# A transformer block on one core: the front rewritten as a list of 140 steps, with several query projections open at once

## The chip, the core and the metric

The kernel runs on one core of one Trainium2 chip. The metric is the device time of one execution in microseconds (us), the median of several runs. One profiled execution gives the trace; its engines are called PE (the matrix engine), PEld (its weight loads), DVE (vector), ACT (scalar), POOL (GpSimd) and SP (which issues most DMAs).

## The reference

One pre-norm block on x of 2048 rows and 448 columns: attention with 16 query heads of 28 columns that share one key and one value head, then a gated FFN of 1792 columns.

```python
x = A_x
h = x + _A_ref(_layernorm(x), wq, wk, wv, wo)
# q = x@wq (16 heads), k = x@wk, v = x@wv, p = softmax(q k / sqrt(28)), (p v) @ wo
h2 = h + _B_ref(_layernorm(h), w1, w3, w2)
# (silu(x@w1) * (x@w3)) @ w2
```

## The kernel before, in words

Everything is computed in a split form: a value is a high part (fp32r) and a low part (the rest), and a product is three matmuls, high by high, low by high, high by low. For 448 rows of contraction that makes 11 matmuls of 512 columns a projection (`mm_D`): three high by high, three low by high, three high by low, and two for the last 64 rows.

x is cut into four quarters t of 512 rows, each of four blocks n of 128 rows. The **front**, of which this case is, does for each quarter: statistics on DVE (`stats`), the power -0.5 on POOL (`ln_rstd`), the scaling (`ln_norm`, on DVE or, with a bias that POOL prepares, on ACT), a small copy on POOL, 16 transposes on PE (`ln_tr`, four chunks c, one PSUM bank each; ACT copies the high part out, DVE subtracts for the low part), one joint projection for key and value (`kv`), and four query projections g (`q(t, g)`), one for four heads. ACT copies a finished projection to SBUF (tile QR); `q(0, 0)` goes straight to the tile QS with a DVE subtraction. `va` transposes the values back; `k_low` makes the keys' low part; `k_diff` on POOL subtracts the keys of neighbouring quarters (tile kd). The query weight is split in four chunks: its high part on ACT, its low part on POOL (`split_wq`, `low_wq`).

Between the projections stand 20 **quads**: the row maxima of the scores for the first steps of the attention. A quad is four matmuls of 32 rows side by side into four banks. A quad "D" multiplies with kd, and ACT writes its relu to SBUF; the quad "U" after it multiplies with the keys KH, and DVE adds the relu and takes the maximum (`both`, line 281). So a pair D, U covers two quarters of the keys for four heads.

There are eight PSUM banks, given out first freed, first taken (`bank`, `done`). ACT, DVE and POOL run what stands in the program in its order, so the order in which the code is written is the order on each of them, and PE waits wherever its next bank, weight or moving operand is not there. In the kernel before, the order is written as calls: `kv` and `q` run their 11 matmuls in one go, with at most one quad after the sixth (`between`).

After the front comes the **main loop** (attention, 256 steps), and then the FFN. `load_wo` clears a tile and loads the output weight; `split_wo` splits it in steps 1, 3, 5 and 7 of the main loop.

Of the kernel before, what the change touches and what calls it, by code (L numbers as in the profile page):

```python
# [38 lines left out]

@with_exitstack  # L40
def block_kernel(
# [98 lines left out]

    def mm_D(ps, lhs, rhs, lsl, rsl, between=None, part=False, lows_last=False):


# [4 lines left out]
        if lows_last:  # L150
            terms.insert(6, terms.pop(9))
        for k, (a, ca, b, cb) in enumerate(terms):
            pe.matmul(  # L153
                ps, lhs[b][:, cb, lsl], rhs[a][:, ca, rsl],
                start=(k == 0), stop=(k == len(terms) - 1 and not part),
            )
            if between is not None and k == 5:
                between()
# [34 lines left out]
    def ln_norm(t, n, eng=ve):  # L193
        _, mv, rs, xns, nb = LN[t]
        xn = xns[n] = ln_pool.tile([P, 512], F32, name="xn", bufs=4)
        if eng is se:
            se.activation(xn[:, :D], X[t][:, n], AF.Identity, bias=nb[:, n : n + 1], scale=rs[:, n : n + 1])
        else:
            eng.tensor_scalar(xn[:, :D], X[t][:, n], mv[:, n, 0:1], rs[:, n : n + 1],
                              op0=ALU.subtract, op1=ALU.mult)  # L200
# [4 lines left out]
    def ln_tr(t, c, ffn=False, dve=False, between=None):  # L205

        ps = bank()
        if c == 0:
            XT[t] = (xt_pool.tile([P, 4, T], F32R, name="xh"), xt_pool.tile([P, 4, T], F32R, name="xl"))
        xh, xl = XT[t]  # L210
        xns = LN[t][3]
        for n in range(NQ):
            pe.transpose(ps[:, n * P : (n + 1) * P], xns[n][:, c * P : (c + 1) * P], ident)  # L213
            if between is not None and n < NQ - 1:
                between()

        def copy(o, i):
            if dve:
                ve.tensor_copy(o, i)
            else:  # L220
                se.activation(o, i, AF.Copy)
# [8 lines left out]
        if c < 3:  # L230
            ve.tensor_tensor(xl[:, c], ps, f(xh[:, c]), op=ALU.subtract)
        else:
            ve.tensor_tensor(xh[64:128, 3], ps[64:128], f(hi[64:128, 3]), op=ALU.subtract)
# [211 lines left out]
    def low_wq(c0, c1, eng):
        for c in range(c0, c1 + 1):
            eng.tensor_tensor(WQ[1][:, c, :, :DH], wq4[:, c], f(WQ[0][:, c, :, :DH]), op=ALU.subtract)

    def split_wq(c0, c1, eng=None):
        for c in range(c0, c1 + 1):  # L450
            se.activation(WQ[0][:, c, :, :DH], wq4[:, c], AF.Copy)
            if eng:
                low_wq(c, c, eng)
# [16 lines left out]
    def norm(t, eng):  # L470
        for n in range(NQ):
            ln_norm(t, n, eng)

    def tr(t, *cs):
        for c in cs or range(4):
            ln_tr(t, c)

    def kv(t, between=None):
        cols = slice(t * T, (t + 1) * T)
        ps = bank()  # L480
        mm_D(ps[:96], WKV, XT[t], slice(0, 96), slice(0, T), between)
        se.activation(KH[0:64, cols], ps[0:64], AF.Identity, bias=kb)
        vt = VT[:, t % 2]
        se.activation(vt[64:96], ps[64:96], AF.Copy)
        sy.dma_start(f(KH[64:128, cols]), f(KH[0:64, cols]))
        return vt, ps

    def k_diff(t):
        ge.tensor_tensor(KD[:, t // 2], f(KH[:, t * T : (t + 1) * T]), f(KH[:, (t - 1) * T : t * T]),
                         op=ALU.subtract)  # L490

    def k_low(t, ps):
        cols = slice(t * T, (t + 1) * T)
        ve.scalar_tensor_tensor(KL[0:64, cols], ps[0:64], kb, f(KH[0:64, cols]), op0=ALU.add, op1=ALU.subtract)
        sy.dma_start(f(KL[64:128, cols]), f(KL[0:64, cols]))
        done(ps)

    def va(t, vt):
        ps = bank()
        for n in range(NQ):  # L500
            pe.transpose(ps[:, 32 * n : 32 * n + 32], vt[64:96, n * P : (n + 1) * P], ident[64:96, 64:96])
# [4 lines left out]
    def q(t, g, between=None):
        ps = bank()
        mm_D(ps, [w[:, :, 4 * g : 4 * g + 4].rearrange("p c h r -> p c (h r)") for w in WQ],
             XT[t], slice(0, P), slice(0, T), between, lows_last=True)
        if t == g == 0:  # L510
            build_qs(0, ps)
        else:
            se.activation(QR[t][:, g], ps, AF.Copy)
        done(ps)

    first = [(quad, i, n, 0, diff) for i, n in ((0, 0), (0, 1), (0, 2), (0, 3), (1, 0)) for diff in (True, False)]
    first += [(quad, 0, n, 1, diff) for n in range(NQ) for diff in (True, False)]
    first += [(max_done, 0), (max_out, 0)]
    first += [(quad, 1, 0, 1, diff) for diff in (True, False)]

    def quads(n=1):
        while n > 0 and first:
            fn, *args = first.pop(0)
            fn(*args)
            n -= fn is quad
# [10 lines left out]
    tr(0, 1, 2, 3)
    split_wq(0, 3)
    low_wq(0, 3, ge)
    v0, p0 = kv(0)
    stats(1)  # L540
    k_low(0, p0)
# [5 lines left out]
    stats(2)
    k_diff(1)
    k_low(1, p1)
    q(0, 2)  # L550
    norm(2, ve)
    q(0, 3)
    va(0, v0)
    va(1, v1)
    build_qs(1)
    quads()
    q(1, 0, quads)
    quads()
    tr(2)
    v2, p2 = kv(2, quads)  # L560
    stats(3, True)
    quads()
    q(1, 1, quads)
# [1 line left out]
    k_low(2, p2)
    va(2, v2)
    quads()
    q(1, 2, quads)
    quads()
    q(1, 3)  # L570
    build_qs(2)
    quads()
    tr(3)
    v3, p3 = kv(3)
    k_diff(3)
# [1 line left out]
    q(2, 0)
    k_low(3, p3)
    va(3, v3)
    q(2, 1)  # L580
    for t, g in ((2, 2), (2, 3), (3, 0), (3, 1)):
        quads()
        q(t, g, quads)
    quads()
    q(3, 2, quads)
    q(3, 3)
    quads(64)
# [227 lines left out]
```

## Time and profile before

| | |
|---|---|
| median of three runs | 1194.07 us (1192.97 to 1194.17) |
| the profiled execution's own time | 1192.15 us |
| its span in the trace | 1190.4 us |
| mean granted clock of PE | 1.00 |
| PE, first key and value projection starts | 11.40 us |
| PE, first matmul of the main loop starts | 90.06 us |

A line of the timeline has start, length, engine, source line, operation, output and inputs, and a count of equal instructions that follow one another; in brackets the idle time before it and what ended it. The lengths of matmuls are modelled and overlap, so the pace of PE is read from start to start.

### The profile page before, as it was taken

The numbers are of one execution on the slowest core, as the hardware profiler recorded it, in microseconds if no ns is written. First come the engines' busy times: TensorE is split into PE (matmuls) and PEld (weight loads), VectorE is DVE, ScalarE is ACT, GpSimd is POOL, SyncE is SP. The second block draws the span as 40 slices with busy tenths as digits, with TensorE's granted clock in tenths as the row PEclk, the third lists the DMA queues.
The fourth block names the chain that finished last, engine by engine and source line by source line (L and its number), as shares of the span: only waits on it lengthen the run. The fifth ranks groups of instructions, "written<-read, shape, count | busy, mean of one in ns | idle before, by whom it ended". The sixth has DMA issues, their size and how long they took to land. (4 is left out here: it accounts for less than half of the span.)

```text
span 1190.4 us, 24122 instructions
## 1 busy us (share of the span) xinstructions
PE 1175.1 (99%) x9594; PEld 727.5 (61%) x9594; DVE 812.0 (68%) x1482; ACT 726.3 (61%) x1381; POOL 332.5 (28%) x258
## 2 busy tenths in 40 slices
PE   9999999999999999999999999999999999999998
PEld 7564444445544445444445443688888888888886
DVE  7758999998898997899997982254444445444333
ACT  4759999997799996899996999411211111111111
POOL 4201101110101110110111032363555455445552
PEclk9999999999999999999999999999999999999999
DMA  5010101000001000010000010114000000000000
GB/s 174 12 37 2 34 2 47 11 12 2 10 13 36 11 12 2 11 46 10 4 12 10 3 46 11 40 45 117 1 32 1 1 1 31 1 1 32 1 1 32
DMA packets 32377, 26.92 MB, mean 23 GB/s; under 512 B 10824, under 2 KB 28936, under 8 KB 32264
## 3 DMA queue, kind: packets, MB, share of 16 engines
q1 hardware_dynamic: 31704, 25.32, 7.2%
q8 instruction: 75, 1.23, 0.4%
q14 instruction: 38, 0.31, 0.1%
q10 hardware_dynamic: 560, 0.06, 0.0%
HBM read 20.25 MB, written 3.80 MB: 20 GB/s over the span
## 5 line engine op out<-in xcount | busy, mean ns | idle before, releaser
L328 ACT ACTIVATE pt<-pb 128x512 f32<-128x512 f32 x1024 | 531.7, 612 | 11.3 <-PE pb L318 6.0
L273 DVE TENSOR_REDUCE mx<-pa 128x1 f32<-128x512 f32 x708 | 461.0, 684 | 52.8 <-PE pb L318 37.0
L318 PE MATMUL pb<-qs,KH 32*128 32x512 f32 x2048 | 342.9, 431 | 0.1
L267 PE MATMUL pa<-KH,qs 32*128 32x512 f32 x866 | 327.4, 487 | 0.4 <-ACT relu L277 0.4
L336 PE MATMUL po<-pt,VA 128*32 128x256 f32 (+1 forms) x2984 | 298.1, 471 | 5.7 <-ACT OT L340 5.3
L318 PE MATMUL pb<-qs,KL 32*128 32x512 f32 x1024 | 283.6, 419 | 0.0
L318 PEld LDWEIGHTS pb<-qs,KH 32*128 32x128 f32 x2048 | 174.5, 182 | 113.7 <-DVE mx L273 49.8
L153 PE MATMUL pa<-xh,w 128*128 128x512 f32 x784 | 202.1, 391 | 0.0
L707 ACT ACTIVATE rb<-pa 128x512 f32<-128x512 f32 x56 | 30.5, 596 | 251.3 <-PE pa L699 251.3
L153 PEld LDWEIGHTS pa<-xh,w 128*128 128x128 f32 x784 | 146.1, 188 | 30.3 <-issue 1.2
L267 PEld LDWEIGHTS pa<-KH,qs 32*128 32x128 f32 x866 | 142.2, 181 | 10.7 <-issue 2.4
L724 PE MATMUL pb<-w2s,hid 128*128 128x448 f32 x672 | 143.9, 370 | 0.7 <-POOL w2s L390 0.7
L318 PEld LDWEIGHTS pb<-qs,KL 32*128 32x128 f32 x1024 | 136.9, 182 | 2.5
L724 PEld LDWEIGHTS pb<-w2s,hid 128*128 128x128 f32 x672 | 123.9, 188 | 20.4 <-issue 10.1
L336 PEld LDWEIGHTS po<-pt,VA 128*32 128x32 f32 x2984 | 58.8, 108 | 122.1 <-issue 104.9
L277 ACT ACTIVATE relu<-pa 128x512 f32<-128x512 f32 x158 | 91.1, 600 | 52.7 <-PE pa L267 34.0
L281 DVE CUSTOM_DVE_ANT_0 relu<-pa,relu 128x512 f32<-128x512 f32 x158 | 105.6, 682 | 16.3 <-ACT relu L277 12.9
L382 POOL TENSOR_TENSOR w<-QR,w 128x1024 fp32r<-128x1024 f32 x32 | 84.3, 2647 | 94.4 <-PE pa L699 80.8
L716 DVE TENSOR_TENSOR hid<-rb,hid 128x512 fp32r<-128x512 f32 x56 | 72.5, 1295 | 39.2 <-ACT hid L715 39.2
L360 POOL TENSOR_TENSOR OT<-OT,rb 128x512 f32<-128x512 f32 x16 | 20.5, 1283 | 274.3 <-DMA rb<-sd 81.3
L153 PE MATMUL pa<-xl,w 128*128 128x512 f32 x336 | 94.6, 390 | 0.0
L381 DVE CAST w<-QR 128x1024 fp32r<-128x1024 f32 x32 | 22.2, 694 | 90.2 <-PE pa L153 82.0
(99 smaller groups left out, 954.9 us busy)
## 6 DMA issues: line engine op xcount, KB each, us to landing
rb<-sd SPq DMA_DIRECT2D x64, 64.0 KB
QR<-in_B_w_dram SPq DMA_DIRECT2D x16, 192.0 KB
X<-in_A_x_dram SPq DMA_DIRECT2D x3, 896.0 KB
...
qs<-ngt SPq DMA_DIRECT2D x64, 2.0 KB
sm<-OT SPq DMA_DIRECT2D x64, 2.0 KB
```

The source lines that it names most:

```text
L153: pe.matmul(ps, lhs[b][:, cb, lsl], rhs[a][:, ca, rsl], start=(k == 0), stop=(k == len(terms) - 1 and not part),)
L267: pe.matmul(self.ps, QS[i][r, 0, n * P : (n + 1) * P], ks[r], start=True, stop=True)
L273: ve.tensor_reduce(self.col(), self.ps, axis=AX.X, op=ALU.max)
L277: se.activation(r, self.ps, AF.Relu)
L281: ve.tensor_tensor_reduce(r, self.ps, r, 1.0, LOW, op0=ALU.add, op1=ALU.max, accum_out=self.col())
L318: pe.matmul(self.ps, (KH, KH, KL)[k][r, c * P : (c + 1) * P], QS[i][r, (0, 1, 0)[k]], start=(k == 0), stop=(k == 2))
L328: se.activation(pt, self.ps, AF.Exp, bias=0.0, scale=SCALE)
L336: pe.matmul(PO[i][32 * j : 32 * j + 32, q], VA[:, c], PT[i, c, j][:, q], start=(c == 0 and h0 == 0), stop=(c == NC - 1 and h1 == 2))
L382: ge.tensor_tensor(wl, W13[k], f(wh), op=ALU.subtract)
L707: se.activation(sg, ps[0], AF.Silu)
L716: ve.tensor_tensor(h[:, 1], sg, f(h[:, 0]), op=ALU.subtract)
L724: pe.matmul(Y[t][n][:, :D], hid[a][:, n * P : (n + 1) * P], w2s[:, b, :D], start=(k == 0 and m == 0), stop=(k == NF - 1 and m == 2))
```

## The change

The front after the first chunk of the first quarter's transposes is written as one list, `FRONT`, whose names call small functions: `tr.t.c` the transposes of a chunk, `wh`, `wp`, `wv` the split of the query weight (high on ACT, low on POOL, low on DVE), `ka.t` and `kb.t` the first six and the last five matmuls of a key and value projection, `qa.t.g` and `qb.t.g` the same of a query projection, `st` statistics, `na` and `nm` the scaling on ACT and on DVE, `kl`, `kd`, `va`, `qs` as before, `D` and `U` the quads, `mx` the maxima of the first four heads. A projection takes its bank at `qa` and keeps it until ACT has copied it out after `qb`. The matmuls themselves and their number are the same.

```diff
+FRONT = """
+tr.0.1 tr.0.2 tr.0.3 wh.1 wh.0 ka.0 wp.0 wh.2 wp.1 st.1.1 kb.0 wh.3 wv.3 na.1.0 na.1.1 wv.2 qa.0.0
+na.1.2 qa.0.1 na.1.3 st.2.1 qa.0.2 qb.0.0 qa.0.3 qb.0.2 qb.0.3 tr.1.0 tr.1.1 tr.1.2 tr.1.3 na.2.0
...
-    def mm_D(ps, lhs, rhs, lsl, rsl, between=None, part=False, lows_last=False):
+    def mm_D(ps, lhs, rhs, lsl, rsl, part=False, lows_last=False, half=None):
...
+            if half is None or half == (k > 5):
+                pe.matmul(
...
+    def wq_high(c):
+        se.activation(WQ[0][:, c, :, :DH], wq4[:, c], AF.Copy)
+
+    def wq_low(eng, c):
+        eng.tensor_tensor(WQ[1][:, c, :, :DH], wq4[:, c], f(WQ[0][:, c, :, :DH]), op=ALU.subtract)
...
+    def q(half, t, g):
+        if not half:
+            PP[t, g] = bank()
+        ps = PP[t, g]
         mm_D(ps, [w[:, :, 4 * g : 4 * g + 4].rearrange("p c h r -> p c (h r)") for w in WQ],
-             XT[t], slice(0, P), slice(0, T), between, lows_last=True)
...
+             XT[t], slice(0, P), slice(0, T), lows_last=True, half=half)
+        if half:
...
+            done(PP.pop((t, g)))
...
+        "tr": ln_tr, "st": stats, "nm": ln_norm, "na": lambda t, n: ln_norm(t, n, se), "np": lambda t, n: ln_norm(t, n, ge),
+        "wh": wq_high, "wp": lambda c: wq_low(ge, c), "wv": lambda c: wq_low(ve, c),
+        "ka": lambda t: kv(False, t), "kb": lambda t: kv(True, t), "kl": k_low, "kd": k_diff, "va": va,
+        "qa": lambda t, g: q(False, t, g), "qb": lambda t, g: q(True, t, g), "qs": build_qs,
...
-    norm(1, ve)
-    q(0, 0)
-    q(0, 1)
-    tr(1)
-    v1, p1 = kv(1)
...
-    norm(3, se)
...
+    for op in FRONT:
+        name, *args = op.split(".")
+        front[name](*map(int, args))
     load_wo()
...
-        at(1 + 2 * g, split_wo, g)
+        at(5 + 2 * g, split_wo, g)
```

On PE, behind the first key and value projection, stood the query projections of the first quarter one whole after the other. The rows give output bank and inputs; xh and xl are the high and low part of the transposed x, OS0 and OS1 those of the query weight, and the number behind pb tells one bank's use from another's.

```order
L153 MATMUL pb_311<-xh_208,OS0_103 128x512 x3
L153 MATMUL pb_311<-xl_209,OS0_103 128x512 x3
L153 MATMUL pb_311<-xh_208,OS0_103 128x512
L153 MATMUL pb_311<-xh_208,OS1_104 128x512 x4
L153 MATMUL pb_326<-xh_208,OS0_103 128x512 x3
L153 MATMUL pb_326<-xl_209,OS0_103 128x512 x3
L153 MATMUL pb_326<-xh_208,OS0_103 128x512
L153 MATMUL pb_326<-xh_208,OS1_104 128x512 x4
```

The same place on PE now:

```order
L164 MATMUL pb_305<-xh_208,OS0_103 128x512 x3
L164 MATMUL pb_305<-xl_209,OS0_103 128x512 x3
L164 MATMUL pb_315<-xh_208,OS0_103 128x512 x3
L164 MATMUL pb_315<-xl_209,OS0_103 128x512 x3
L164 MATMUL pb_340<-xh_208,OS0_103 128x512 x3
L164 MATMUL pb_340<-xl_209,OS0_103 128x512 x3
L164 MATMUL pb_305<-xh_208,OS0_103 128x512
L164 MATMUL pb_305<-xh_208,OS1_104 128x512 x4
L164 MATMUL pb_355<-xh_208,OS0_103 128x512 x3
L164 MATMUL pb_355<-xl_209,OS0_103 128x512 x3
L164 MATMUL pb_340<-xh_208,OS0_103 128x512
L164 MATMUL pb_340<-xh_208,OS1_104 128x512 x4
```

Three projections are begun, 18 matmuls, before the first matmul that reads the low part of the weight.

On ACT, from the first key copy (KH) to the second quarter's first high part (the second xh), stood:

```order
L482 ACTIVATE KH_93<-pb_269,small_85 64x512
L484 ACTIVATE vt_118<-pb_269 32x512
L248 ACTIVATE qs_323<-pb_311 128x512
L513 ACTIVATE QR0_96<-pb_326 128x512
L221 ACTIVATE xh_340<-pb_339 128x512
```

and stands now, with the scaling of the second quarter (xn, from X1) and one chunk of the weight (OS0):

```order
L484 ACTIVATE KH_93<-pb_263,small_85 64x512
L486 ACTIVATE vt_118<-pb_263 32x512
L455 ACTIVATE OS0_103<-OT_102 128x16x28
L206 ACTIVATE xn_298<-X1_78,rs_273 128x448
L206 ACTIVATE xn_301<-X1_78,rs_273 128x448
L206 ACTIVATE xn_312<-X1_78,rs_273 128x448
L206 ACTIVATE xn_322<-X1_78,rs_273 128x448
L257 ACTIVATE qs_352<-pb_305 128x512
L517 ACTIVATE QR0_96<-pb_340 128x512
L517 ACTIVATE QR0_96<-pb_355 128x512
L230 ACTIVATE xh_375<-pb_374 128x512
```

The four scalings stand ahead of the copies that free the banks of the projections; their bias (rs) comes from POOL. The third quarter is scaled on ACT too, between its other work, and the fourth, which was scaled on ACT, is scaled on DVE.

On PE, the last quarter's transposes (xn to pb) stood behind a U quad (KH, qs) and ahead of the key and value projection (wkvs):

```order
L267 MATMUL pa<-KH,qs 128x512 x4
L213 MATMUL pb<-ident,xn 128x128 x16
L153 MATMUL pb<-xh,wkvs 96x512 x3
L153 MATMUL pb<-xl,wkvs 96x512 x3
L153 MATMUL pb<-xh,wkvs 96x512 x5
L153 MATMUL pb<-xh,OS_103 128x512 x3
```

They stand now so, where the first wkvs projection is that of the third quarter and the second that of the fourth:

```order
L276 MATMUL pa<-KH,qs 128x512 x4
L502 MATMUL pb<-ident,vt 128x32 x4
L222 MATMUL pb<-ident,xn 128x128 x12
L164 MATMUL pb<-xh,wkvs 96x512 x3
L164 MATMUL pb<-xl,wkvs 96x512 x3
L222 MATMUL pb<-ident,xn 128x128 x4
L164 MATMUL pb<-xh,wkvs 96x512 x5
L276 MATMUL pa<-kd,qs 128x512 x4
L164 MATMUL pb<-xh,wkvs 96x512 x3
L164 MATMUL pb<-xl,wkvs 96x512 x3
L164 MATMUL pb<-xh,wkvs 96x512 x5
```

Between the last quarter's transposes and the projection that reads them now stand a projection of another quarter and a D quad.

More of the change, by code (lines that the diff above doesn't have):

```diff
@@ L37 @@
               "6a 7a 5c 4a 4b 6b 7b").split()
+FRONT = """
+tr.0.1 tr.0.2 tr.0.3 wh.1 wh.0 ka.0 wp.0 wh.2 wp.1 st.1.1 kb.0 wh.3 wv.3 na.1.0 na.1.1 wv.2 qa.0.0
+na.1.2 qa.0.1 na.1.3 st.2.1 qa.0.2 qb.0.0 qa.0.3 qb.0.2 qb.0.3 tr.1.0 tr.1.1 tr.1.2 tr.1.3 na.2.0
+qb.0.1 ka.1 na.2.1 qs.2 na.2.2 kb.1 na.2.3 qa.1.0 kl.0 st.3 qa.1.2 tr.2.0 tr.2.1 tr.2.2 tr.2.3
+qb.1.2 kd.1 nm.3.0 qb.1.0 nm.3.1 va.1 D.0.0.0 kl.1 qa.1.1 U.0.0.0 qb.1.1 nm.3.2 D.0.1.0 qa.1.3
+nm.3.3 U.0.1.0 qb.1.3 D.0.2.0 qa.2.0 U.0.2.0 qs.1 va.0 tr.3.0 tr.3.1 tr.3.2 ka.2 tr.3.3 kb.2 kl.2
+D.0.3.0 ka.3 kb.3 kl.3 kd.3 qb.2.0 U.0.3.0 qa.2.3 D.1.0.0 qb.2.3 U.1.0.0 qa.3.2 D.0.0.1 qb.3.2
+U.0.0.1 qa.3.1 D.0.1.1 qb.3.1 U.0.1.1 qa.3.3 D.0.2.1 qb.3.3 U.0.2.1 qa.2.1 D.0.3.1 qb.2.1 U.0.3.1
+mx.0 qa.3.0 va.3 D.1.0.1 qb.3.0 va.2 U.1.0.1 qa.2.2 qb.2.2
+""".split()
 @with_exitstack
@@ L152, in mm_D @@
         for k, (a, ca, b, cb) in enumerate(terms):
[L153 to L158, printed above, removed]
+            if half is None or half == (k > 5):
+                pe.matmul(
+                    ps, lhs[b][:, cb, lsl], rhs[a][:, ca, rsl],
+                    start=(k == 0), stop=(k == len(terms) - 1 and not part),
+                )
     def load_w(dst, w, eng=sy):
@@ L443, in block_kernel @@
     wq4 = wq_r.rearrange("p c (h r) -> p c h r", h=H)
[L445 to L453, printed above, removed]
+    def wq_high(c):
+        se.activation(WQ[0][:, c, :, :DH], wq4[:, c], AF.Copy)
+    def wq_low(eng, c):
+        eng.tensor_tensor(WQ[1][:, c, :, :DH], wq4[:, c], f(WQ[0][:, c, :, :DH]), op=ALU.subtract)
     def load_wo():
@@ L468, in stats, with kv @@
         ln_rstd(t, nbias=nbias)
[L470 to L486, printed above, removed]
+    PP, VV = {}, {}
+    def kv(half, t):
+        if not half:
+            PP[t] = bank()
+        ps = PP[t]
+        mm_D(ps[:96], WKV, XT[t], slice(0, 96), slice(0, T), half=half)
+        if half:
+            cols = slice(t * T, (t + 1) * T)
+            se.activation(KH[0:64, cols], ps[0:64], AF.Identity, bias=kb)
+            vt = VV[t] = VT[:, t % 2]
+            se.activation(vt[64:96], ps[64:96], AF.Copy)
+            sy.dma_start(f(KH[64:128, cols]), f(KH[0:64, cols]))
     def k_diff(t):
@@ L490, in k_diff, with k_low @@
                          op=ALU.subtract)
-    def k_low(t, ps):
-        cols = slice(t * T, (t + 1) * T)
+    def k_low(t):
+        cols, ps = slice(t * T, (t + 1) * T), PP.pop(t)
         ve.scalar_tensor_tensor(KL[0:64, cols], ps[0:64], kb, f(KH[0:64, cols]), op0=ALU.add, op1=ALU.subtract)
@@ L496, in k_low, with va @@
         done(ps)
-    def va(t, vt):
-        ps = bank()
+    def va(t):
+        ps, vt = bank(), VV.pop(t)
         for n in range(NQ):
@@ L504, in va, with maxima @@
         done(ps)
-    def q(t, g, between=None):
-        ps = bank()
+    def q(half, t, g):
+        if not half:
+            PP[t, g] = bank()
+        ps = PP[t, g]
         mm_D(ps, [w[:, :, 4 * g : 4 * g + 4].rearrange("p c h r -> p c (h r)") for w in WQ],
-             XT[t], slice(0, P), slice(0, T), between, lows_last=True)
[L510 to L525, printed above, removed]
+             XT[t], slice(0, P), slice(0, T), lows_last=True, half=half)
+        if half:
+            if t == g == 0:
+                build_qs(0, ps)
+            else:
+                se.activation(QR[t][:, g], ps, AF.Copy)
+            done(PP.pop((t, g)))
+    def maxima(i):
+        max_done(i)
+        max_out(i)
+    front = {
+        "tr": ln_tr, "st": stats, "nm": ln_norm, "na": lambda t, n: ln_norm(t, n, se), "np": lambda t, n: ln_norm(t, n, ge),
+        "wh": wq_high, "wp": lambda c: wq_low(ge, c), "wv": lambda c: wq_low(ve, c),
+        "ka": lambda t: kv(False, t), "kb": lambda t: kv(True, t), "kl": k_low, "kd": k_diff, "va": va,
+        "qa": lambda t, g: q(False, t, g), "qb": lambda t, g: q(True, t, g), "qs": build_qs,
+        "D": lambda i, n, kp: quad(i, n, kp, True), "U": lambda i, n, kp: quad(i, n, kp, False), "mx": maxima,
+    }
     for n in range(NQ):
@@ L535, in block_kernel @@
     done(warm)
[L536 to L541, printed above, removed]
-    norm(1, ve)
-    q(0, 0)
-    q(0, 1)
-    tr(1)
-    v1, p1 = kv(1)
[L547 to L563, printed above, removed]
-    norm(3, se)
[L565 to L575, printed above, removed]
-    load_wo()
[L577 to L587, printed above, removed]
+    for op in FRONT:
+        name, *args = op.split(".")
+        front[name](*map(int, args))
+    load_wo()
     free.remove(7)
```

## The prediction

> **What bounds the kernel now.** The page comes first:
>
> ```profile
> span 1190.4 us, 24122 instructions
> PE 1175.1 (99%) x9594; PEld 727.5 (61%) x9594; DVE 812.0 (68%) x1482; ACT 726.3 (61%) x1381; POOL 332.5 (28%) x258
> ```
>
> PE is the bound, but 99% overstates it, since the lengths of matmuls overlap. So I read PE's timeline of the front from start to start, first where nothing else seems to hold it up, for prices, then where it stands.
>
> ```profile
> 14.41 0.84 PE L153 MATMUL pb<-xh,OS 128*128 128x512 f32 x3
> ...
> 17.50 1.20 PE L153 MATMUL pb<-xh,OS 128*128 128x512 f32 x4 [0.60 <-POOL OS L447]
> ...
> 20.36 1.91 PE L213 MATMUL pb<-ident,xn 128*128 128x128 f32 x16
> 22.02 1.12 PE L153 MATMUL pb<-xh,wkvs 128*96 128x512 f32 x3
> ...
> 30.16 0.49 PE L501 MATMUL pb<-ident,vt 32*128 32x32 f32 x5
> ...
> 37.67 1.45 PE L153 MATMUL pb<-xh,wkvs 128*96 128x512 f32 x3 [0.65 <-ACT xh L221]
> ...
> 41.75 0.50 PE L267 MATMUL pa<-kd,qs 32*128 32x512 f32 x4
> ...
> 46.89 1.72 PE L267 MATMUL pa<-kd,qs 32*128 32x512 f32 x3 [0.28 <-DVE mx L281]
> ...
> 51.18 0.50 PE L267 MATMUL pa<-KH,qs 32*128 32x512 f32 x1 [0.37 <-ACT relu L277]
> ...
> 52.99 0.51 PE L267 MATMUL pa<-kd,qs 32*128 32x512 f32 x4
> ...
> 60.00 1.67 PE L153 MATMUL pb<-xl,wkvs 128*96 128x512 f32 x3 [0.60 <-DVE xl L231]
> ...
> 62.66 0.85 PE L153 MATMUL pb<-xh,OS 128*128 128x512 f32 x3
> ...
> 65.25 0.43 PE L501 MATMUL pb<-ident,vt 32*128 32x32 f32 x4
> 65.61 0.97 PE L153 MATMUL pb<-xh,OS 128*128 128x512 f32 x3
> ...
> 68.35 0.50 PE L267 MATMUL pa<-kd,qs 32*128 32x512 f32 x4
> ...
> 70.39 0.51 PE L267 MATMUL pa<-KH,qs 32*128 32x512 f32 x4
> ...
> 74.23 0.51 PE L267 MATMUL pa<-KH,qs 32*128 32x512 f32 x4
> ...
> 90.06 0.49 PE L267 MATMUL pa<-KH,qs 32*128 32x512 f32 x1
> ```
>
> Prices: the 11 matmuls of a projection take 65.25 - 62.66 = 2.59 us, 0.235 each; 16 transposes 22.02 - 20.36 = 1.66; a value transpose (`va`) 65.61 - 65.25 = 0.36. From 70.39 to 74.23 stand 11 matmuls and two quads, so a quad costs (3.84 - 2.59) / 2 = 0.625.
>
> Now the stretches, time taken less work at these prices. 14.41 to 20.36, 22 matmuls: 5.95 - 5.17 = 0.78. To 30.16, 16 transposes and 33 matmuls: 9.80 - 9.42 = 0.38. To 41.75, two `va`, four quads, 22 matmuls, 16 transposes: 11.59 - 10.05 = 1.54. To 52.99, four quads, one `va`, 22 matmuls: 11.24 - 8.03 = 3.21. To 62.66, two quads, 16 transposes, 22 matmuls: 9.67 - 8.08 = 1.59. To 68.35, 22 matmuls and a `va`: 0.16. To 90.06, ten quads and 66 matmuls: -0.05. So PE stands 7.6 us in the front, nearly all before 62.66, and the last third is dense. That is all a new order of the front can win: its work stays the same.
>
> **The change part by part.** PE's work from 14.41 on: 209 matmuls x 0.235 = 49.1, 48 transposes 5.0, four `va` 1.4, 20 quads 12.5, in all 68.0. If PE never waits, the main loop starts at 14.41 + 68.0 = 82.4 instead of 90.06. I follow the new list along PE at these prices and ask at each place whether what it needs is there. The rows for the other engines:
>
> ```profile
> 21.05 2.06 ACT L221 ACTIVATE xh<-pb 128x512 fp32r<-128x512 f32 x4
> 31.28 2.05 ACT L277 ACTIVATE relu<-pa 128x512 f32<-128x512 f32 x4
> 47.93 2.72 ACT L197 ACTIVATE xn<-X,rs 128x448 f32<-128x448 f32 x4 [1.11 <-POOL rs L191]
> ```
>
> ```profile
> 12.97 4.48 POOL L447 TENSOR_TENSOR OS<-OT,OS 128x448 fp32r<-128x448 f32 x4 [2.05 <-ACT OS L451]
> 46.27 1.01 POOL L188 TENSOR_TENSOR rs<-rs,small 128x4 f32<-128x4 f32 x1 [13.23 <-DVE rs L187]
> 65.92 1.29 POOL L489 TENSOR_TENSOR kd<-KH 128x512 fp32r<-128x512 f32 x1 [7.17 <-DMA KH<-KH]
> ...
> 95.42 1.14 POOL L463 TENSOR_TENSOR WO<-OT,WO 128x448 fp32r<-128x448 f32 x1 [26.68 <-DVE WO L462]
> ```
>
> ```profile
> 13.65 0.63 DVE L182 BATCH_NORM_STATS2 st<-X 128x6 f32<-128x448 f32 x1
> ...
> 16.71 0.76 DVE L187 TENSOR_SCALAR rs<-mv 128x4 f32<-128x4 f32 x1
> ...
> 21.67 1.89 DVE L231 TENSOR_TENSOR xl<-pb,xh 128x512 fp32r<-128x512 f32 x3 [0.69 <-ACT xh L221]
> 23.59 0.69 DVE L233 TENSOR_TENSOR xh<-pb,xh 64x512 fp32r<-64x512 f32 x1
> ...
> 28.68 2.74 DVE L199 TENSOR_SCALAR xn<-X,mv,rs 128x448 f32<-128x448 f32 x4 [0.36 <-POOL rs L188]
> ...
> 74.86 0.69 DVE L281 CUSTOM_DVE_ANT_0 relu<-pa,relu 128x512 f32<-128x512 f32 x1 [1.31 <-ACT relu L277]
> ...
> 75.48 0.69 DVE L281 CUSTOM_DVE_ANT_0 relu<-pa,relu 128x512 f32<-128x512 f32 x1
> ...
> 94.95 0.39 DVE L462 CAST WO<-OT 128x448 fp32r<-128x448 f32 x1
> ```
>
> ```profile
> 63.57 0.46 SPq L485 DMA_DIRECT2D KH<-KH  x1
> ```
>
> *The weight's low part (0.78 before).* POOL made its four chunks one after the other, 1.12 us each, and PE waited. Now 18 matmuls (4.2 us) go first, to 18.6. POOL begins half a us later than its 12.97, with the second chunk that ACT makes, and its two end at about 15.7. DVE's two stand behind the statistics (13.65 to 16.71) and the small operation after them, at about 16.9. Their duration no row shows for this form; the same operation with both inputs in SBUF elsewhere:
>
> ```profile
> L716 DVE TENSOR_TENSOR hid<-rb,hid x56: 691/1242/2718, 767.8 to 1179.0; 128x512 fp32r<-128x512 f32 x56
> ```
>
> For 448 columns that is 0.60 to 2.38, by the median 1.09 us. I take the median, because POOL works beside it here as there: done at 19.1, needed at 18.6 + 3 x 0.235 = 19.3, so nothing is lost. At the upper end they are done at 21.7 and PE loses 2.4 us.
>
> The rows show DVE held up by POOL: the scalar operation at 16.71 took 0.76 us and ended with POOL's last chunk (12.97 + 4.48 = 17.45), and four scalings at 28.68 took 2.74. [...]
>
> *The scaling of the second and third quarter on ACT.* Its bias leaves POOL 47.93 - 46.27 = 1.66 us after the power starts, so ACT scales from 16.9 + 1.7 = 18.6 to 21.25 (four in 2.65). Behind it in ACT's queue wait the copies of q(0, 0), q(0, 2), q(0, 3). Who waits for those: the transposes `tr.1.3` take q(0, 0)'s bank at 24.8, which DVE releases at about 23.1, behind the third quarter's statistics (19.1 + 3.1, then two operations). And `tr.1.0` needs the scaled rows at 23.6. So 1.7 us of slack; beyond that every us of delay is one on PE. The third quarter's last scaling ends at 31.2, its transposes start at 31.8.
>
> *Second quarter's transposes (0.38 before).* The last half of a projection, 1.2 us, now lies between them and `ka.1`; ACT (four chunks in 2.06) and DVE (0.63 a chunk) are done in time.
>
> *Third quarter (1.54 and most of 3.21 before).* Here quads, transposes and statistics met: between 30.16 and 52.99 DVE had sixteen `both` (75.48 - 74.86 = 0.62 each), 3.1 us of statistics (13.65 to 16.71) and 2.6 of low parts (1.89 + 0.69) to do, and quads waited for its banks. Now the statistics of the last quarter and the third's transposes (31.8 to 33.5) come before the first quad (36.2), behind them two half projections. POOL's kd for it is ready at 34.
>
> *Fourth quarter (1.59 before).* The transposes come at 47; between them and `ka.3` at 52 lie 2.6 us of `ka.2` and `kb.2` and a quad, while DVE, busy with a U quad's four `both` (from 46.7) and a copy until 49.4, finishes the low parts at 51.4. This is tight: `ka.2` needs a bank that DVE frees at about 48.0, just when PE comes. I allow 0.5 us. The keys' copy by DMA takes 65.92 - 63.57 = 2.35 us; kd is ready near 59, the quad that needs it comes at 61.
>
> *Last third.* One projection and two quads in 3.84 us, as before: ACT needs five operations of about 0.5 and DVE 4 x 0.62 = 2.5 of that, and DVE idles 1.31 a pair. Nothing changes; the steps before it only come earlier.
>
> *The output weight's load and split* go behind the front; main-loop steps 5 to 11 instead of 1 to 7 still come before the tile is overwritten in step 16. I cost this at nothing; DVE and POOL do 4 x 0.39 and 4 x 1.14 us of it beside PE. Without that cover it would cost a PE wait of one such split, 1.1 us.
>
> Sum: 7.6 us of waits go, 0.6 come back (0.5 at the fourth quarter, 0.1 at the low parts): 7.0. Against the profiled execution's 1192.15 us that is 1185.2; the three runs' median is 1.9 above that execution, so 1194.07 - 7.0 = 1187.1. A measurement of this kernel can tell about 0.2% (2.4 us) from no change.
>
> **The rivals.** *Half of it comes back (faster still).* The tight places all miss: low parts 2.4, ACT's scaling 1, the fourth quarter's chain 1.2. Then 7.6 - 4.6 = 3.0 is won: 1191.1. For it: margins of 0.2 to 1.7 us on durations from other places. Against: the first two depend on DVE being at its slowest.
>
> *The main loop takes it back.* If its first steps wait for DVE, which does its last `both` 1.2 us closer to it (11 matmuls behind the last U quad instead of 16), a gain would end there: 1192 to 1196, taken as 1193.5. Against: DVE stood idle before its first reduction there:
>
> ```profile
> 90.59 3.84 DVE L273 TENSOR_REDUCE mx<-pa 128x1 f32<-128x512 f32 x6 [1.69 <-PE pa L267]
> ```
>
> 1.69 us covers 1.2, and nothing later hangs on a fixed time.
>
> *Slower: the quads run out of banks.* One or two projections hold a bank while each quad takes four of eight; `U.0.0.1` takes the bank that `U.1.0.0`'s last `both` frees, only 0.4 us ahead by my count. If each of 20 quads waited one `both` (0.62), 12.4 us come against the 7.6: 1194.07 + 4.8 = 1198.9. The break-even is 0.38 us a quad (7.6 / 20); slower by over 0.2% it is from 0.5 on. Against: a pair of D and U takes nine banks in turn before and after alike, and the dense stretch before shows DVE idle in each pair.
>
> **How the numbers follow.** Forecast 0.68, its own range 1185.6 to 1188.9; half back 0.18; taken back 0.09; slower 0.05. Faster by over 0.2% are the first two, 0.86; the third is within 0.2%: 0.09; slower 0.05. The range goes from 1185.0 (all 7.6 us, and 1.5 more if 209 matmuls are priced 0.007 us too high) to 1192.0, which takes in the half.
>
> **What would show it.** Right: PE's first main-loop matmul at 82.5 to 83.5 us, no bracketed wait of PE in the front over 0.5 us, the first low-part matmul about 18.6 without a wait, the last third again at 3.84 a pair, and the main loop as long as before (1190.4 - 90.06 = 1100.3). Wrong: PE waiting for DVE's OS or for ACT's xn at 19 to 25 (the first rival's terms), pairs of quads longer than 4.2 us, or a main loop longer by what the front saved.

## The result, and the profile after

| | before | after |
|---|---|---|
| median | 1193.52 us (1192.73 to 1194.17, 4 runs) | 1183.36 us (1183.27 to 1183.48, 4 runs) |
| profiled execution, own time / span | 1192.15 / 1190.4 us | 1183.29 / 1181.5 us |
| first query projection starts | 14.41 us | 14.05 us |
| main loop's first matmul | 90.06 us | 81.16 us |
| from there to the end of the span | 1100.3 us | 1100.3 us |

The ratio is 0.992, with a 95% interval from 0.9908 to 0.9931: faster, and by more than forecast (1187.1, range 1185.0 to 1192.0). By their times, two of the four executions of before in the table (1194.07 and 1194.17) are of a slower kind that the new kernel does not show and that the experiments take up. (The list has 111 names; the title's 140 is a miscount.)

The page of after, its first lines:

```profile
span 1181.5 us, 24119 instructions
PE 1169.5 (99%) x9594; PEld 726.5 (61%) x9594; DVE 809.2 (68%) x1480; ACT 729.5 (62%) x1385; POOL 330.0 (28%) x258
```

PE's timeline of after, columns as before (start, length, engine, line, operation, tiles, count):

```profile
14.05 0.85 PE L164 MATMUL pb<-xh,OS 128*128 128x512 f32 x3
...
18.14 1.98 PE L164 MATMUL pb<-xh,OS 128*128 128x512 f32 x8
...
22.90 1.91 PE L222 MATMUL pb<-ident,xn 128*128 128x128 f32 x16
24.57 1.40 PE L164 MATMUL pb<-xh,OS 128*128 128x512 f32 x5
...
45.78 1.53 PE L222 MATMUL pb<-ident,xn 128*128 128x128 f32 x12
47.14 0.95 PE L164 MATMUL pb<-xh,wkvs 128*96 128x512 f32 x3
...
50.73 0.94 PE L164 MATMUL pb<-xh,wkvs 128*96 128x512 f32 x3
...
60.45 0.50 PE L276 MATMUL pa<-kd,qs 32*128 32x512 f32 x4
...
64.27 0.50 PE L276 MATMUL pa<-kd,qs 32*128 32x512 f32 x4
...
81.16 0.50 PE L276 MATMUL pa<-KH,qs 32*128 32x512 f32 x1
```

No row between 14 and 82 us ends in a bracket, where before had five. The second of the eight matmuls at 18.14 is the first that reads the low part of the weight, and nothing holds it up. The front took 81.16 - 14.05 = 67.11 us against 75.65: PE is dense from end to end. The other engines at the places that the prediction walks through, first ACT of after:

```profile
18.61 2.72 ACT L206 ACTIVATE xn<-X,rs 128x448 f32<-128x448 f32 x4 [2.40 <-POOL rs L200]
21.35 0.60 ACT L257 ACTIVATE qs<-pb 128x512 fp32r<-128x512 f32 x1
```

DVE of after:

```profile
16.45 1.16 DVE L458 TENSOR_TENSOR OS<-OT,OS 128x448 fp32r<-128x448 f32 x2
...
48.41 1.88 DVE L240 TENSOR_TENSOR xl<-pb,xh 128x512 fp32r<-128x512 f32 x3
```

POOL of after:

```profile
16.59 1.36 POOL L197 TENSOR_TENSOR rs<-rs,small 128x4 f32<-128x4 f32 x1 [1.26 <-DVE rs L196]
...
21.59 1.04 POOL L197 TENSOR_TENSOR rs<-rs,small 128x4 f32<-128x4 f32 x1
```

DVE's two low parts end at 17.6 (forecast 19.1; PE comes to them at about 18.8); ACT's scaling starts at 18.6, as walked; the last quarter's low parts end at 50.3, ahead of the projection at 50.73.

### The profile page after: what moved, and what is told of

Read it like the earlier page. It is cut to its first block, busy times and chain, and to the rows that moved or that the text cites. A ratio compares the mean times of both kernels' runs of the same rounds, so it can differ in the third digit from the quotient of the medians.

```text
span 1181.5 us, 24119 instructions
## 1 busy us (share of the span) xinstructions
PE 1169.5 (99%) x9594; PEld 726.5 (61%) x9594; DVE 809.2 (68%) x1480; ACT 729.5 (62%) x1385; POOL 330.0 (28%) x258
```

## The experiments

Theory W (waits) is the prediction's: the gain is what PE stood in the front, each stand can be given back by itself, and they add up. Its rivals are that one part carries most of it: B, the projections that are open side by side; S, the scaling that moved to ACT. Theory C came up on the way: behind a stand, PE's granted clock falls, so a stand costs more than its length. All kernels were timed beside the kernel before, whose median was 1192.48 to 1192.63 in the four groups of runs. "Front" below is the time from the first query projection to the main loop, which the new kernel does in 67.11 us; where the front begins differs by up to 1.0 us between profiled executions (13.90 to 14.87), so it is the surer measure of the two. In the cuts, lines of the list show the names round the place that changes; the list's own line breaks are not kept.

**The old order, written as a list (list_old).** The change's writing, with the order, the engines and the steps of the output weight as before.

```diff
-tr.0.1 tr.0.2 tr.0.3 wh.1 wh.0 ka.0 wp.0 wh.2 wp.1 st.1.1 kb.0 wh.3 wv.3 na.1.0 na.1.1 wv.2 qa.0.0
+tr.0.1 tr.0.2 tr.0.3 wh.0 wh.1 wh.2 wh.3 wp.0 wp.1 wp.2 wp.3 ka.0 kb.0 st.1 kl.0 nm.1.0 nm.1.1 nm.1.2 nm.1.3
+qa.0.0 qb.0.0 qa.0.1 qb.0.1 tr.1.0 tr.1.1 tr.1.2 tr.1.3 ka.1 kb.1 st.2 kd.1 kl.1 qa.0.2 qb.0.2
...
-        at(5 + 2 * g, split_wo, g)
+        at(1 + 2 * g, split_wo, g)
```

> The old order written as a list: the same instructions in the same order on every engine as before. If the waits of PE make the difference (theory W), the time is that of before, 1193.5 us within its own spread of 1.5, and the first query projection to the main loop takes 75.6 us on PE again. If the list or its halves as such pay, it is faster. If part of the 10.2 us lies in how before's runs differ (its profiled run was 1.4 us under its median), this run's trace shows where: a later start of the first projection, or a longer wait in the front, with the main loop at 1100.3 us.

1192.43 us (11 runs), ratio 1.000 (0.9991 to 1.0009); the front took 75.89 us. The way of writing is worth nothing; the order is the change.

**Parts undone, one at a time.** *back_first*: the first quarter's projections whole, all low parts on POOL, the second quarter's scaling on DVE.

```diff
-tr.0.1 tr.0.2 tr.0.3 wh.1 wh.0 ka.0 wp.0 wh.2 wp.1 st.1.1 kb.0 wh.3 wv.3 na.1.0 na.1.1 wv.2 qa.0.0
-na.1.2 qa.0.1 na.1.3 st.2.1 qa.0.2 qb.0.0 qa.0.3 qb.0.2 qb.0.3 tr.1.0 tr.1.1 tr.1.2 tr.1.3 na.2.0
+tr.0.1 tr.0.2 tr.0.3 wh.0 wh.1 wh.2 wh.3 wp.0 wp.1 wp.2 wp.3 ka.0 kb.0 st.1 nm.1.0 nm.1.1 nm.1.2 nm.1.3
+qa.0.0 qb.0.0 qa.0.1 qb.0.1 tr.1.0 tr.1.1 tr.1.2 tr.1.3 ka.1 kb.1 st.2.1 qa.0.2 qb.0.2 na.2.0
...
```

> The new list with the first quarter's projections, the second quarter's scaling (on DVE) and transposes put back to the old order, and the weight's low part all on POOL again. Theory W: the first two stretches' waits come back, 0.8 + 0.4 = 1.2 us, so 1184.6 us, and 68.3 us from the first query projection to the main loop instead of 67.1. Theory B (projections open side by side are what pays, in the later part too): less than 0.3 us, as the later part is untouched.

1184.77 us, ratio 0.9931 (0.9919 to 0.9943); the front took 68.45 us, 1.3 more, as theory W expected and more than B allows. The old wait is back, on PE's timeline of back_first:

```profile
17.87 1.20 PE L163 MATMUL pb<-xh,OS 128*128 128x512 f32 x4 [0.60 <-POOL OS L457]
```

*scale_dve*: the second and third quarter scaled on DVE, the last on ACT, as before the change, with the statistics that prepare the bias for ACT moved accordingly; the places in the list stay.

```diff
-tr.0.1 tr.0.2 tr.0.3 wh.1 wh.0 ka.0 wp.0 wh.2 wp.1 st.1.1 kb.0 wh.3 wv.3 na.1.0 na.1.1 wv.2 qa.0.0
+tr.0.1 tr.0.2 tr.0.3 wh.1 wh.0 ka.0 wp.0 wh.2 wp.1 st.1 kb.0 wh.3 wv.3 nm.1.0 nm.1.1 wv.2 qa.0.0
...
```

> The new list, with the second and third quarter scaled by DVE and the fourth by ACT, as before. Theory W: the order hides most of it, DVE is late by about 0.5 us at the low part of the weight and 0.5 at the first quad: 1184.4 us, at most 1185. Rival S (it is the moved scaling that pays): 3 us or more come back, 1186.4 or above.

1185.31 us, ratio 0.9934 (0.9922 to 0.9946); the front took 68.29 us, 1.2 more. The time is 0.3 us above the bound that W gave and 1.1 below that of S. The scalings now stand in DVE's queue ahead of its share of the low parts, and PE waits for those:

```profile
20.10 1.42 PE L163 MATMUL pb<-xh,OS 128*128 128x512 f32 x5 [0.57 <-DVE OS L457]
```

*back_fourth*: the last quarter's transposes straight ahead of its projection, and the D quad behind it.

```diff
-tr.3.0 tr.3.1 tr.3.2 ka.2 tr.3.3 kb.2 kl.2 D.0.3.0 ka.3 kb.3 kl.3 kd.3
+ka.2 kb.2 kl.2 tr.3.0 tr.3.1 tr.3.2 tr.3.3 ka.3 kb.3 kl.3 kd.3 D.0.3.0
```

> The new list, only with the last quarter's 16 transposes straight ahead of the projection that reads them, and the third quarter's key projection ahead of both. Theory W: PE waits for ACT and DVE there as before, 1.6 us, so 1185.0 us. Rival: other work of DVE made that wait before, and it is gone now: under 0.5 us.

1185.86 us, ratio 0.9939 (0.9927 to 0.9952); the front took 68.80 us, 1.7 more, about the term that the prediction had read for this place (1.59). On PE's timeline of back_fourth the projection waits again and runs thinly, six matmuls in 53.39 - 51.13 = 2.26 us:

```profile
51.13 1.45 PE L163 MATMUL pb<-xh,wkvs 128*96 128x512 f32 x3 [0.26 <-ACT xh L229]
...
53.39 1.31 PE L163 MATMUL pb<-xh,wkvs 128*96 128x512 f32 x5
```

The median is 2.5 above the new kernel's, more than the 1.6 expected; in the profiled execution 0.56 of the difference is a later start (14.61 against 14.05).

So three parts, each undone alone, give back 1.2 to 1.7 us of front, and none carries the gain. That speaks for W. No run puts the third quarter's transposes alone back between the quads, where the two largest waits stood together with the statistics (1.54 and 3.21); that they went is read from the new timeline. W holds until the opposite is tried:

*new_first*: the new list up to the second quarter's projection, then the old order, with the third quarter scaled on DVE and the last on ACT and the output weight's steps as before.

```diff
 qa.0.2 qb.0.0 qa.0.3 qb.0.2 qb.0.3 tr.1.0 tr.1.1 tr.1.2 tr.1.3 qb.0.1 ka.1 kb.1
-qa.1.0 kl.0 st.3 qa.1.2 tr.2.0 tr.2.1 tr.2.2 tr.2.3 qb.1.2 kd.1 nm.3.0 qb.1.0 nm.3.1 va.1 D.0.0.0
+kl.0 kd.1 kl.1 nm.2.0 nm.2.1 nm.2.2 nm.2.3 va.0 va.1 qs.1 D.0.0.0 qa.1.0 U.0.0.0 qb.1.0 D.0.1.0
...
```

> The new list as far as the second quarter's key projection, and from there the old order, with the third quarter scaled on DVE and the fourth on ACT as before. Before's runs fell into two groups, at about 1192.1 us with a mean granted clock of 0.998 to 1.000 and at about 1194.2 with 0.997; the new kernel and three lists near it have shown the first group alone. Theory W: the later waits of 6.3 us stay, so about 8.8 - 1.2 = 7.6 us above the new kernel in the faster group, 1190.8. Theory C (the low clock comes from PE standing in the third and fourth quarter's stretches): two groups again, 2 us apart. Rival (the low clock comes from the start): one group.

1197.36 us, ratio 1.0038 (1.0026 to 1.0051): slower than the kernel before, where W expected 1190.8. W is wrong in that the parts add up. With the first quarter's projections used up early, nothing is left to lie between the second quarter's keys and the quad that needs their difference; PE's timeline of new_first:

```profile
33.36 0.70 PE L275 MATMUL pa<-kd,qs 32*128 32x512 f32 x4 [2.73 <-POOL kd L489]
```

and POOL's, where kd itself had waited for the keys' copy:

```profile
31.95 1.36 POOL L489 TENSOR_TENSOR kd<-KH 128x512 fp32r<-128x512 f32 x1 [8.42 <-DMA KH<-KH]
```

In the new list two halves of projections, 16 transposes and two more halves stand there. The front took 82.17 us, 6.5 more than before; the clock fell as well, in two places of its windows (start and end of each stretch of 4 us, its length, busy time of PE, PEld, DVE, ACT and POOL, PE's granted clock, use of the DMA engines and GB/s):

```profile
34.00:38.00 4.00, 4.00 (x17) 2.63 (x14) 0.06 (x1) 2.06 (x4) 1.42 (x3) 0.64 0.00 0
54.00:58.00 4.00, 4.00 (x12) 2.33 (x10) 2.14 (x7) 2.79 (x6) 0.48 (x2) 0.50 0.15 35
```

The 0.64 and the 0.50 are PE's granted clock. Read as full or half, which low_pool's finer windows below show, the windows from 30 to 62 us (0.94 and 0.64, later 0.50 and 0.65, the others 1.00) make 3.4 us at half from 33.5 and 6.8 us from 54.0. The five executions fall apart, as C expected: two at 1196.6 to 1196.7 with a mean clock of 0.999, three at 1197.4 to 1199.0 with 0.996 to 0.997. Even the first are 5.8 us above W's figure, so the clock is not the whole of it. What a fall has to do with a wait is taken up with low_pool.

**Where the low part of the weight is made.** *low_pool*: DVE's two chunks on POOL, at the same places of the list.

```diff
-wh.3 wv.3 na.1.0 na.1.1 wv.2 qa.0.0
+wh.3 wp.3 na.1.0 na.1.1 wp.2 qa.0.0
```

> The new list with all four chunks of the weight's low part on POOL. By the walk along the list POOL is done at about 17.6 us, ahead of the first need at 18.6, and the second quarter's bias is about 0.9 us later, within 1.7 us of slack: the same as the new kernel within 0.3 us. Rival (DVE's two chunks are what removed the first wait): 0.6 to 0.8 us slower.

1187.18 us, ratio 0.9948 (0.9935 to 0.996): 3.8 us above the new kernel, where I had expected none, having overlooked that these places lie behind the power in POOL's queue. POOL of low_pool, the power and then the two chunks:

```profile
16.52 1.02 POOL L196 TENSOR_TENSOR rs<-rs,small 128x4 f32<-128x4 f32 x1 [0.86 <-DVE rs L195]
...
18.13 1.15 POOL L457 TENSOR_TENSOR OS<-OT,OS 128x448 fp32r<-128x448 f32 x1
...
19.86 1.13 POOL L457 TENSOR_TENSOR OS<-OT,OS 128x448 fp32r<-128x448 f32 x1
```

PE's timeline of low_pool:

```profile
18.03 0.84 PE L163 MATMUL pb<-xh,OS 128*128 128x512 f32 x3
21.05 2.14 PE L163 MATMUL pb<-xh,OS 128*128 128x512 f32 x5 [2.17 <-POOL OS L457]
22.99 1.49 PE L163 MATMUL pb<-xl,OS 128*128 128x512 f32 x3
```

The wait is 2.17 us, but the front grew by 71.18 - 67.11 = 4.07. The three matmuls at 22.99 took 24.27 - 22.99 = 1.28 us to the next row's start instead of 0.68. The windows of low_pool show why:

```profile
19.00:21.00 2.00, 0.00 (x0) 0.00 (x0) 0.50 (x3) 1.91 (x3) 1.80 (x5) 1.00 0.00 0
21.00:23.00 2.00, 1.95 (x6) 1.53 (x7) 0.42 (x1) 0.60 (x1) 1.79 (x5) 0.62 0.00 0
23.00:25.00 2.00, 2.00 (x6) 1.62 (x5) 0.27 (x1) 0.00 (x0) 0.00 (x0) 0.52 0.00 0
```

In windows of one us the clock reads 1.00 up to 21, then 0.75, 0.50, 0.50 and 0.54, and 1.00 again from 25 on. That fits a clock that is either full or half, and was at half for (1 - 0.62) x 2 / 0.5 = 1.5 us and then 1.9 us, 3.4 together, which costs 1.7 us of work: 2.2 + 1.7 = 3.9 of the 4.07. This is theory C. By time and mean clock, not every execution of low_pool falls: two of the five, at 1.0, took 1186.3 to 1186.4, the three at 0.999, the traced one among them, took 1187.2. *low_fill* puts 18 idle transposes (1.9 us) into that wait, ahead of the projection's second half:

```diff
-qa.0.2 qb.0.0 qa.0.3
+qa.0.2 hx.18 qb.0.0 qa.0.3
...
+    def fill(n):
+        ps = bank()
+        for _ in range(n):
+            pe.transpose(ps[:, :P], ident, ident)
+        done(ps)
```

> low_pool, where PE waits 2.2 us for POOL's third and fourth chunk and then shows a granted clock of 0.5 for 3.4 us, with 18 idle transposes (1.9 us, results unused) put on PE ahead of that wait. Theory C (standing PE lowers its clock, and that costs again what the wait cost): the wait shrinks to 0.3 us, no low clock follows, and the time is 1.6 us below low_pool, 1185.6. Rival (the clock drops for another reason, or the filler only adds to PE's work): 1187.2 or more.

1185.83 us, ratio 0.9943 (0.993 to 0.9955): 1.35 us faster than low_pool, with more work on PE, and each of its five executions below each of low_pool's; the front took 69.57 us, 1.6 less. PE's timeline of low_fill has 0.18 us of the wait left:

```profile
18.44 2.13 PE L479 MATMUL pb<-ident 128*128 128x128 f32 x18
20.32 0.95 PE L163 MATMUL pb<-xh,OS 128*128 128x512 f32 x3
21.45 1.44 PE L163 MATMUL pb<-xh,OS 128*128 128x512 f32 x5 [0.18 <-POOL OS L457]
```

The mean granted clock of its traced execution is 1.0, where 3.4 us at half would make it 0.999, and its three matmuls behind the wait took 23.40 - 22.72 = 0.68 us again, not 1.28. Here a stand filled with idle work was cheaper than an empty one. *low_pool2* keeps all four chunks on POOL but ahead of the power:

```diff
-wp.0 wh.2 wp.1 st.1.1 kb.0 wh.3 wv.3 na.1.0 na.1.1 wv.2
+wp.0 wh.2 wp.1 wh.3 wp.2 wp.3 st.1.1 kb.0 na.1.0 na.1.1
```

> All four chunks of the weight's low part on POOL, as in low_pool, but ahead of the power and its bias in POOL's queue (and the high part's four in a row on ACT). Theory W (it was the place in POOL's queue, not the engine): chunks done at 17.7 us, bias at 19.2, within the slack of 1.7 us, so the new kernel's time, 1183.4 within 0.4 us. Rival (POOL cannot do all four in time): PE waits at 18 to 20 us and the time is 1 us or more above.

1183.44 us, ratio 0.9924 (0.9911 to 0.9936), front 67.13: the same as the new kernel. POOL of low_pool2 makes the four in 4.5 us, and the power comes behind them:

```profile
13.82 4.51 POOL L457 TENSOR_TENSOR OS<-OT,OS 128x448 fp32r<-128x448 f32 x4 [2.96 <-ACT OS L454]
18.29 1.01 POOL L196 TENSOR_TENSOR rs<-rs,small 128x4 f32<-128x4 f32 x1
```

For these chunks the place in the queue counts, not the engine; the 18 matmuls put ahead cover POOL's whole series.

**The last quarter's statistics late (stats_late).**

```diff
-qa.1.0 kl.0 st.3 qa.1.2 tr.2.0 tr.2.1 tr.2.2 tr.2.3 qb.1.2 kd.1 nm.3.0 qb.1.0 nm.3.1
+qa.1.0 kl.0 qa.1.2 tr.2.0 tr.2.1 tr.2.2 tr.2.3 qb.1.2 kd.1 qb.1.0
...
+U.0.1.0 st.3 nm.3.0 nm.3.1 nm.3.2 nm.3.3 qb.1.3
```

> The new list, only with the last quarter's statistics and scalings put between the first quads, behind the second U, as before. Theory W: DVE then owes 3.1 us there and frees the quads' banks late, so 1 to 3 us of PE waits come back: 1184.4 to 1186.4 us. Rival (the transposes between the quads made the old wait, the statistics did not): under 0.5 us.

1190.11 us, ratio 0.9973 (0.9962 to 0.9983): 6.8 us came back, where 1 to 3 were expected, and by another way. PE waits for the late scaling itself, not for the quads' banks; PE's timeline of stats_late:

```profile
50.26 3.36 PE L221 MATMUL pb<-ident,xn 128*128 128x128 f32 x12 [3.59 <-DVE xn L207]
53.27 1.63 PE L163 MATMUL pb<-xh,wkvs 128*96 128x512 f32 x3
```

and its windows:

```profile
48.00:50.00 2.00, 0.00 (x0) 0.00 (x0) 0.79 (x4) 0.00 (x0) 1.03 (x1) 0.57 0.00 0
50.00:52.00 2.00, 1.74 (x6) 1.11 (x7) 2.00 (x7) 0.05 (x1) 1.64 (x5) 0.50 0.00 0
52.00:54.00 2.00, 2.00 (x10) 1.85 (x9) 2.00 (x8) 1.49 (x3) 0.99 (x1) 0.50 0.02 4
54.00:56.00 2.00, 2.00 (x11) 1.42 (x9) 1.80 (x4) 0.26 (x1) 0.00 (x0) 0.72 0.00 0
```

A wait of 3.59 us made the front 73.26 - 67.11 = 6.15 longer; the clock stood at half for 1.7 + 2 + 2 + 1.1 = 6.8 us, from 48.3 on, so the first 2 of them inside the wait. It fell 1.6 us after PE had stopped at 46.7. The 4.9 us behind the wait cost 2.4 of work, and 3.6 + 2.4 is nearly all. Of the single moves tried this is the dearest; the statistics' early place is what keeps the last quarter from it.

**One bank fewer for the front (bank7).**

```diff
+    for k in range(1):
+        held.append(free.pop(0))
     for op in FRONT:
...
+    free.extend(held)
```

> The new list with one of the eight banks held out of the front. Theory W with the walk's margin of 0.4 us at the quads' banks: a quad then takes a bank that was freed one step later, so 20 quads wait up to 0.3 us each, 2 to 6 us in all: 1185.4 to 1189.4. If the banks are not near their limit: under 1 us. If they were the bound already: 8 us or more.

1186.09 us, ratio 0.9941 (0.9927 to 0.9955), front 69.36: an eighth of the banks costs 2.25 us of front, 0.11 a quad, within what was expected. The rival in which the quads run out of banks needed 0.38 a quad with all eight; the list is not near that edge.

**Fewer idle transposes at the start (heat24).**

```diff
-    heat(30)
+    heat(24)
```

> The new kernel with 24 instead of 30 idle transposes at the start. The first projection started between 13.95 and 14.87 us in the runs so far. If PE's idle transposes at the lower pace set that, it starts at or under 14.0 and the time is 0 to 0.6 us below the new kernel, 1183.0. If they are needed to raise the pace, the first projections take longer and it is slower by 0.5 us or more.

1183.14 us (1182.93 to 1183.45), ratio 0.9921 (0.9907 to 0.9935). Its range overlaps the new kernel's (1183.27 to 1183.48); no better version is shown.

**Why the kernel before has slower executions.** Over all groups of runs the old order was executed 65 times: 20 at a mean clock of 0.997 (1193.9 to 1195.1 us), 45 at 0.998 to 1.0 (1191.8 to 1194.0). Four more executions of it, list_old with nothing but a comment added, were traced to catch one of the first kind:

```diff
-SCALE = DH ** -0.5
+SCALE = DH ** -0.5  # look1
```

> The old order again, for a trace of the slower group (about four runs in ten: 1194 us, mean granted clock 0.997). Theory C: a stretch with a granted clock of about 0.5, some 3.4 us long, right behind the longest standing of PE in the front, at 46 to 52 us; nothing of it in a run at 1192 us. Rival: the low clock lies at the start or in the main loop.

> The old order written as a list, one look for its trace. If it falls in the slower group (about 1194.3 us, 0.4 of the executions so far), theory C (the clock falls behind a thin stretch of PE) expects a granted clock of .5 to .9 for some 3.5 us in the front, between 46 and 62 us, where PE stood 3.2 and then 1.6 us, and the main loop's start about 2 us later than 90.0. The rival (the slower group has nothing to do with the front) expects full clock up to 90 us and the loss somewhere in the main loop or the FFN. In the faster group: 1192.0 us and full clock throughout.

> As the look before it: either 1192.0 us with full clock, or 1194.3 us with, by theory C, the clock at .5 to .9 for some 3.5 us between 46 and 62 us.

> As the two looks before it: either 1192.0 us with full clock, or 1194.3 us with, by theory C, the clock at .5 to .9 for some 3.5 us between 46 and 62 us.

They took 1191.94, 1194.10, 1192.85 and 1192.68 us. The second is of that kind; PE's timeline of old_look2:

```profile
47.35 2.01 PE L275 MATMUL pa<-kd,qs 32*128 32x512 f32 x3 [0.27 <-DVE mx L289]
49.29 1.65 PE L163 MATMUL pb<-xh,OS 128*128 128x512 f32 x3
50.73 1.48 PE L163 MATMUL pb<-xl,OS 128*128 128x512 f32 x3
...
92.20 0.49 PE L275 MATMUL pa<-KH,qs 32*128 32x512 f32 x1
```

and its windows:

```profile
46.00:48.00 2.00, 1.61 (x10) 0.73 (x8) 1.93 (x8) 0.60 (x1) 1.20 (x2) 1.00 0.00 0
48.00:50.00 2.00, 2.00 (x4) 1.04 (x5) 1.96 (x6) 1.61 (x3) 0.63 (x4) 0.52 0.00 0
50.00:52.00 2.00, 2.00 (x6) 1.20 (x4) 0.00 (x0) 2.00 (x5) 0.57 (x3) 0.50 0.30 70
52.00:54.00 2.00, 2.00 (x8) 1.23 (x8) 0.92 (x3) 1.03 (x3) 0.00 (x0) 0.50 0.00 0
54.00:56.00 2.00, 2.00 (x10) 1.11 (x9) 1.62 (x6) 0.74 (x2) 0.00 (x0) 0.77 0.00 0
```

The clock falls at about 48 us, in the very stretch where PE stood most (3.21 us from 41.75 to 52.99), stays at half for 1.9 + 2 + 2 + 0.9 = 6.8 us, and the front takes 92.20 - 14.80 = 77.40 us instead of 75.65. The profiled executions of before, list_old and old_look1 (1192.15, 1191.84 and 1191.94 us) show 1.00 in these windows. The third and the fourth lie between: the front takes 76.60 and 76.53 us. In the third the clock falls in the same stretch, for 3.4 us; windows of old_look3:

```profile
42.00:46.00 4.00, 4.00 (x19) 2.43 (x19) 3.86 (x12) 3.34 (x6) 0.00 (x0) 1.00 0.15 35
46.00:50.00 4.00, 3.37 (x13) 1.79 (x12) 3.63 (x12) 2.51 (x4) 1.93 (x5) 0.85 0.00 0
50.00:54.00 4.00, 4.00 (x18) 2.23 (x16) 1.43 (x5) 2.91 (x7) 0.47 (x2) 0.73 0.15 35
```

For the fourth I have the pace alone: the six matmuls in that stretch take 51.31 - 48.47 = 2.84 us, like 51.74 - 48.88 = 2.86 in the third, where six in front of it take 1.58 in both; I count it as 3.4 us too. So the six traced executions of the old order are of three kinds, with 0, 3.4 and 6.8 us at half clock, each step worth 0.8 to 0.9 us of front. *old_fill* puts six idle transposes ahead of each of three projections of the second quarter, two of them in that stretch and one just behind it, into the bank that the projection overwrites:

```diff
             PP[t, g] = bank()
+            if (t, g) in ((1, 1), (1, 2), (1, 3)):
+                for _ in range(6):
+                    pe.transpose(PP[t, g][:, :P], ident, ident)
```

> The old order with six idle transposes (0.6 us) ahead of each of three query projections of the second quarter, in the stretch where PE stood 3.2 us, into the bank that the projection overwrites. Theory C (thin PE makes the clock fall) expects no execution in the slower group: all between 1191.8 and 1193.6 us, median 1192.0 to 1193.0, so as fast as the old order's median or up to 0.8 us faster although PE does 18 transposes more. The rival (the groups are not the front's) expects the two groups again, each later by what of the 1.9 us of transposes the waits do not hide: median 1192.5 to 1195.

1193.12 us (1192.42 to 1193.86, 11 runs), ratio 1.0002 (0.9993 to 1.0011). Its mean clock was 0.999 or 1.0 in all eleven; beside it, four of 15 executions of before were at 0.997, up to 1194.57. At 4 in 15, none in eleven would come by chance about three times in a hundred; so the long fall seems to go, as C has it, for 1.9 us of extra work on PE, and the median is 0.5 higher, less than the interval can tell. It is not all as C expected: the median is 0.1 above its interval and inside the rival's (1192.5 to 1195), and five of the eleven, at 1193.6 to 1193.9 and 0.999, still lie apart from the rest. A single fall as in old_look3 would fit them, but none of the five was traced, and the traced one, at 1192.42, shows 1.00 as before does.

## Why the prediction was too small

The mechanism was right for the whole change: the waits went, and nothing came back. What failed is the size, in two steps that make the 3.7 us between forecast and median. The first alone put the time outside the range, by 1.6 us: the lower end takes in 7.6 + 1.5 = 9.1 us of gain, and 8.86 came between the two profiled executions.

*The step to the median: "the three runs' median is 1.9 above that execution, so 1194.07 - 7.0".* It carries the 1.9 us over to the new kernel, as if they belonged to the measurement. They belong to the old order, and to the draw: before's median stood 1194.07 - 1192.15 = 1.92 above its profiled execution, the new one's 1183.36 - 1183.29 = 0.07. Half of the miss, 1.85 us. Two of the three executions behind that median have the slower kind's times; in the four later groups of 9 to 15 the median of before was 1192.5 to 1192.6, only 0.3 to 0.5 above the same trace, and 14 of those 50 were at 0.997. From there a gain of 7.0 gives 1185.5, so of the miss 2.1 us would have been left. The old_look2 trace shows an execution in which such an amount is lost in the front, at the place of the largest term (3.21), to a clock at half; whether the same happened in the executions that made up the first median no trace shows. A median that lies 1.9 us off a trace with the clock at 1.00 should have raised the question of what the other executions do in that stretch.

*The sum of 7.0.* Between the two profiled executions 1192.15 - 1183.29 = 8.86 us went, 1.9 more:

- "If PE never waits": it did not, and the front's work is 67.1 us instead of 68.0. So what PE stood before was 75.65 - 67.11 = 8.5 us and not 7.6. The price of 0.235 a matmul was too high: 39 matmuls from 14.05 to 22.90 are 0.227 each, which makes 209 of them 1.7 us cheaper; a quad in the dense part, (3.82 - 11 x 0.227) / 2 = 0.66 instead of 0.625, makes 20 of them 0.7 dearer. Net some 0.9.
- "I allow 0.5 us" for the last quarter and 0.1 for the low parts: not needed, 0.6. The chain at the last quarter holds with 1.2 us to spare (low parts done at 50.3, read from 51.5 on).
- The first query projection began 0.36 earlier, which lies within the spread of that start and is no part of the change.

*What held.* The walk along the engines: ACT's scaling at 18.6, no wait at the first low-part matmul, quads and projections again in 3.82 a pair (64.27 - 60.45), the main loop, though it starts at 81.16 and not at 82.5 to 83.5, as long as before (so the rival in which it takes the gain back is out, and the later output-weight split costs nothing). DVE's chunks took 1.16 us for two, under the bound of 0.60 each, so the upper end that fed the rival "half comes back" was far off. POOL's power, which starts 0.14 us behind DVE's first chunk, took 1.36 us, and the next one (21.59), with no DVE chunk beside it, 1.04. So it was POOL that took longer, by 0.3 us; DVE's second chunk ran on beside the power, DVE's two were done at 17.6, and PE did not wait. The two delays that the prediction reads from the rows of before, 0.76 us for a scalar operation of DVE and 2.74 for four scalings, stand there against 0.17 (27.38) and 1.78 (18.60) for the same operations; that POOL made the difference no run isolates.

*What was wrong though it didn't show in the number.* The prediction treats the stands as separate terms to be collected, which is sound for the whole change, where PE never waits, and not for a part. new_first shows it: the same matmuls that fill one gap are missing from the next, and the first part of the new order alone is slower than none of it.
